# The last sub-tile of an FFT and feed-forward kernel, made in two column halves

## The chip, the cores and the metric

The kernel runs on one core of one Trainium2 chip. The metric is the device time of one execution in microseconds, taken over several runs; lower is better. Beside the timed runs, one execution of each kernel was profiled. The profiled *span*, from the first to the last instruction of the program, is 1.7 to 2.2 us shorter than the time.

## The reference

```python
# x: 8 x 3008 x 256
X = rfft(x, axis=1)
Yr = Xr @ w_r - Xi @ w_i + b_r ;  Yi = Xr @ w_i + Xi @ w_r + b_i
Yr, Yi = soft_threshold(Yr, 0.01), soft_threshold(Yi, 0.01)
y = irfft(Yr + 1j * Yi, n=3008, axis=1).reshape(24064, 256)
h = y @ w_in                       # 256 -> 2048
g = s * relu(h) ** 2 + b
out = g @ w_out                    # 2048 -> 256, float32
```

Only the last line matters here: the end of its last tile of 512 tokens.

## The kernel before

The feed-forward part goes tile by tile, 512 tokens each. The second product of a tile is made sub-tile by sub-tile (128 tokens, 256 output columns, 16 accumulating matmuls). Two sub-tiles share a bank of PSUM (the memory into which TensorE accumulates) and one evacuation (VectorE copies the result from PSUM to SBUF, the on-chip memory, and applies `s` and the bias on the way); a store goes out for each sub-tile. In the last tile, sub-tiles 2 and 3 are already handled alone so that less work hangs on the end.

```python
apool = ctx.enter_context(tc.tile_pool(name="psa", bufs=2, space=bass.MemoryType.PSUM))
opool = ctx.enter_context(tc.tile_pool(name="op", bufs=3))
# ... cut ...
def other_bank():
    return apool.tile([P, 512], F32, name="psa", tag="psa")
# ... cut ...
        if kind == "main":                                   # in store(tl, sub, src)
            rows = out[b * N + 512 * j : b * N + 512 * (j + 1), :]
            rows = rows.rearrange("(n1 n2) d -> n2 n1 d", n2=N2)[8 * sub : 8 * sub + 8]
            nc.sync.dma_start(out=rows, in_=src)
            return
# ... cut ...
        def mm(sub, mc):                                     # in second_mms(ti)
            alone = ti == len(tiles) - 1 and sub >= 2
            h = 0 if alone else sub % 2
            if h == 0 and mc == 0:
                hold["ps"] = other_bank().rearrange("p (h e) -> p h e", h=2)
            ps = hold["ps"]
            nc.tensor.matmul(
                ps[0:size, h, :], gts[(ti, mc // 2)][:, mc % 2, sub * size : (sub + 1) * size],
                w_out_t[:, mc, :],
                start=(mc == 0), stop=(mc == MC - 1),
            )
            # ... cut ...
            if mc == MC - 1 and (alone or h == 1 or sub == nsub - 1):
                k = h + 1
                ost = opool.tile([P, 2, D], F32, name="ost", tag="ost")
                nc.vector.scalar_tensor_tensor(
                    out=ost[0:size, 0:k], in0=ps[0:size, 0:k], scalar=s_bc[0:size],
                    in1=bias_bc[0:size].unsqueeze(1).to_broadcast([size, k, D]), op0=ALU.mult, op1=ALU.add,
                )
                load["dve"] += 0.12 + 0.27 * k
                for i in range(k):
                    store(tl, sub - k + 1 + i, ost[:, i, :])
```

The line to keep in mind is `bufs=3`: evacuated tiles take turns in three buffers of SBUF, and a buffer can be written again only when every store that reads it has landed. The framework in which the kernel is written puts in those waits by itself; nothing in the code shows them.

## Time and profile before

| | before |
|---|---|
| median of 3 runs, before the change was tried | 846.8 us (846.79 to 846.98) |
| profiled span | 844.56 us |
| TensorE busy | 835.1 us, 99% |
| last matmul ends | 840.47 us |
| from there to the end (the *tail*) | 4.10 us |

How to read it: TensorE works without a gap almost to the end, so the only stretch where other engines and the DMA set the time is the tail. The tail is a line of single steps: evacuation of the last sub-tile (VectorE), issue of its store (the SyncE queue, SPq), landing of the store (its last semaphore increment), closing. In the profile lines PE is TensorE, PEld its weight loads, DVE VectorE, DVEq and SPq the instruction queues of VectorE and SyncE. The lines that show this stand in the prediction.

### The profile page before, as it was taken

Reading aid. Unit: us, or ns where it says so; the run is one execution under the profiler, and the core shown is the slowest. Engines: PE = TensorE matmul, PEld = TensorE weight load, DVE = VectorE, ACT = ScalarE, POOL = GpSimd, SP = SyncE. Lnnn points to the kernel's source line nnn. Section 1 sums busy time; section 2 is a strip of 40 time slices with the busy share of each in tenths; the row PEclk is TensorE's granted clock in tenths of the full one; section 3 lists DMA queues with packets and bytes.
Section 4 is the critical chain, followed back from the end, with each engine's and each line's share of the span. In section 5 each row is a group of like instructions: output and inputs, shape, how many; then the busy total and the mean of one; then the engine's idle time right before and its main releaser. Section 6 shows DMA issues by size and latency. Waiting matters only on the chain.

```text
span 844.6 us, 17119 instructions
## 1 busy us (share of the span) xinstructions
PE 835.1 (99%) x6654; PEld 601.3 (71%) x6654; DVE 694.7 (82%) x1034; ACT 640.6 (76%) x862; POOL 45.9 (5%) x73
## 2 busy tenths in 40 slices
PE   8999999999999999999999999999999999999998
PEld 7857767777677766777677776777667777766765
DVE  5999987888888988888888888798978888776674
ACT  5987887778778877788777787778877778666673
POOL 4630000000000001000000000000000000000000
PEclk9999999999999999999999999999999999999999
DMA  7955467224851367324761247613354223411111
GB/s 200 181 151 118 119 161 199 74 77 98 202 156 54 103 171 188 93 70 107 189 174 50 81 101 196 172 43 90 106 152 125 59 78 97 113 33 38 38 44 50
DMA packets 105939, 96.06 MB, mean 114 GB/s; under 512 B 9607, under 2 KB 97675, under 8 KB 104515
## 3 DMA queue, kind: packets, MB, share of 16 engines
q1 hardware_dynamic: 99362, 80.55, 32.9%
q0 software_dynamic: 6496, 14.42, 10.6%
q8 instruction: 52, 0.85, 0.4%
q14 instruction: 29, 0.23, 0.1%
HBM read 53.52 MB, written 46.66 MB: 119 GB/s over the span
## 4 chain that ended last, share of the span: by engine, by line
PE 92%; ACT 3%; DVE 2%; DMA 1%; issue 1%; POOL 0%; DVEq 0%; ACTq 0%; POOLq 0%
PE psa L852 38%; PE psh L781 37%; PE psf L647 4%; PE psf L582 3%; PE psf L633 2%; PE psf L677 2%; PE psf L618 2%; PE psf L730 2%; ACT rt L788 1%; DMA x<-in_x_dram 1%; PE psm L425 1%; POOL x L213 0%; ACT yt L170 0%; DVE z L463 0%; PE psf L456 0%
## 5 line engine op out<-in xcount | busy, mean ns | idle before, releaser
L788 ACT ACTIVATE rt<-psh 128x1024 f32<-128x1024 f32 (+2 forms) x384 | 387.2, 1009 | 120.2 <-PE psh L781 118.8
L795 DVE TENSOR_TENSOR gt<-rt 128x1024 f16<-128x1024 f32 (+2 forms) x319 | 382.3, 1202 | 94.4 <-ACT rt L788 93.4
L852 PE MATMUL psa<-w_out_t,gt 128*128 128x256 f16 (+1 forms) x3024 | 454.4, 272 | 0.1
L852 PEld LDWEIGHTS <-gt 128*128 128x128 f16 (+1 forms) x3024 | 300.9, 101 | 186.6 <-issue 1.1
L781 PE MATMUL psh<-yt,w_in 128*128 128x512 f16 (+1 forms) x1344 | 396.8, 378 | 0.2 <-ACT rt L788 0.2
L781 PEld LDWEIGHTS <-w_in 128*128 128x128 f16 x1536 | 142.7, 98 | 26.2 <-issue 1.2
L862 DVE SCALAR_TENSOR_TENSOR ost<-psa,s_bc,bias_bc 128x512 f32<-128x512 f32 (+2 forms) x97 | 71.1, 733 | 9.6 <-PE psa L852 7.9
L792 ACT ACTIVATE gt<-rt 128x1024 f16<-128x1024 f32 (+2 forms) x65 | 68.2, 1050 | 0.9
L652 DVE TENSOR_TENSOR ring<-psf,s 128x512 f16<-128x512 f32 x84 | 57.6, 685 | 3.3 <-PE psf L647 3.2
L170 ACT CAST v<-psf 128x512 f16<-128x512 f32 x77 | 44.8, 582 | 19.4 <-PE psf L677 19.4
L170 ACT CAST xf<-psf 128x512 f16<-128x512 f32 x79 | 46.3, 586 | 8.8 <-PE psf L618 8.8
L781 PE MATMUL psh<-tail,w_in 128*128 128x512 f16 (+1 forms) x192 | 52.1, 353 | 0.0
L170 ACT CAST u<-psf 96x512 f16<-96x512 f32 x74 | 42.8, 580 | 11.2 <-PE psf L582 10.9
L647 PE MATMUL psf<-W_g,xf 128*128 128x256 f16 x336 | 50.4, 273 | 0.0
L170 ACT CAST yt<-psf 128x480 f16<-128x480 f32 (+2 forms) x76 | 39.0, 520 | 14.7 <-PE psf L730 14.2
L213 POOL DMA_DIRECT2D x<-in_x_dram x36 | 18.8, 527 | 432.9 <-PE psf L582 431.7
L582 PE MATMUL psf<-x,A_t 94*96 94x512 f16 x102 | 38.9, 382 | 1.0 <-ACT yt L170 0.6
L658 DVE TENSOR_TENSOR ring<-ring,high 128x512 f16<-128x512 f16 x84 | 35.6, 423 | 2.3
L659 DVE TENSOR_TENSOR ring<-ring 128x512 f16<-128x512 f16 x84 | 35.6, 423 | 2.1
L657 DVE TENSOR_TENSOR ring<-ring,low 128x512 f16<-128x512 f16 x84 | 35.5, 422 | 1.6
L647 PEld LDWEIGHTS <-xf 128*128 128x128 f16 x336 | 32.9, 98 | 4.1 <-issue 0.2
L730 PE MATMUL psf<-C_t,vs 96*128 96x96 f16 x448 | 33.2, 205 | 0.0
(100 smaller groups left out, 508.6 us busy)
## 6 DMA issues: line engine op xcount, KB each, us to landing
out_dram<-ost SPq DMA_DIRECT2D x152, 128.0 KB
ud<-u SPq DMA_DIRECT2D x28, 384.0 KB
us<-ud SPq DMA_DIRECT2D x28, 384.0 KB
vd<-v SPq DMA_DIRECT2D x42, 256.0 KB
vs<-vd SPq DMA_DIRECT2D x14, 768.0 KB
x<-in_x_dram POOLq DMA_DIRECT2D x28, 376.0 KB, 6.3
ring<-ring SPq DMA_DIRECT2D x280, 32.0 KB
out_dram<-ost SPq DMA_DIRECT2D x16, 120.0 KB
```

Source lines behind the costliest of these rows:

```text
L170: return None, nc.scalar.copy(out=dst, in_=src)
L582: nc.tensor.matmul(ps[0:96, :], A_t[0:N1, :], x16[(b, c)][0:N1, j * D : (j + 2) * D], start=True, stop=True,)
L647: nc.tensor.matmul(ps[:, r, :], xt[:, 2 - r, dc], W_g[:, dc, r], start=(dc == 0), stop=(dc == DC - 1),)
L652: nc.vector.tensor_tensor(out=t, in0=ps, in1=hold[i // 2][:, i % 2].unsqueeze(1).to_broadcast([P, 2, D]), op=ALU.add,)
L658: nc.vector.tensor_tensor(out=m, in0=m, in1=high, op=ALU.min)
L730: nc.tensor.matmul(ps[:, j * 96 : (j + 1) * 96], vs[(b, h)][:, k, ec * P : (ec + 1) * P], C_t, start=True, stop=True,)
L781: nc.tensor.matmul(o, w_in_t[dc][:, mc * P : (mc + 1) * P], r, start=(dc == 0), stop=(dc == DC - 1),)
L788: nc.scalar.activation(out=rt[:, :, 0:w], in_=ps[:, :, 0:w], func=AF.Relu)
L792: nc.scalar.activation(out=gt[:, :, 0:w], in_=rt[:, :, 0:w], func=AF.Square)
L795: nc.vector.tensor_tensor(out=gt[:, :, 0:w], in0=rt[:, :, 0:w], in1=rt[:, :, 0:w], op=ALU.mult)
L852: nc.tensor.matmul(ps[0:size, h, :], gts[(ti, mc // 2)][:, mc % 2, sub * size : (sub + 1) * size], w_out_t[:, mc, :], start=(mc == 0), sto ...
L862: nc.vector.scalar_tensor_tensor(out=ost[0:size, 0:k], in0=ps[0:size, 0:k], scalar=s_bc[0:size], in1=bias_bc[0:size].unsqueeze(1).to_broad ...
```

## The change

The intent is to shorten that line. Sub-tile 3 of the last tile is made in two groups of 128 columns. The first group can be evacuated and stored while the second is still on TensorE, so that after the last matmul only half a sub-tile is left to evacuate and store.

```diff
-    def store(tl, sub, src):
+    def store(tl, sub, src, e=slice(None)):
...
-            nc.sync.dma_start(out=rows, in_=src)
+            nc.sync.dma_start(out=rows[:, :, e], in_=src)
...
+        def mm_last(c, mc):
+            if mc == 0:
+                hold["ps"] = other_bank()
+            ps, sub = hold["ps"], nsub - 1
+            e = slice(c * P, c * P + P)
+            nc.tensor.matmul(
+                ps[0:size, 0:P], gts[(ti, mc // 2)][:, mc % 2, sub * size : (sub + 1) * size],
+                w_out_t[:, mc, e], start=(mc == 0), stop=(mc == MC - 1),
+            )
+            if mc == MC - 1:
+                ost = opool.tile([P, P], F32, name="ost", tag="ost")
+                nc.vector.scalar_tensor_tensor(
+                    out=ost[0:size], in0=ps[0:size, 0:P], scalar=s_bc[0:size],
+                    in1=bias_bc[0:size, e], op0=ALU.mult, op1=ALU.add,
+                )
+                store(tl, sub, ost, e)
+
+        if ti == len(tiles) - 1:
+            units = [lambda s=s, m=m: mm(s, m) for s in range(nsub - 1) for m in range(MC)]
+            return units + [lambda c=c, m=m: mm_last(c, m) for c in range(2) for m in range(MC)]
```

Below, A is the evacuation of sub-tiles 0 and 1 of the last tile (with its stores A1 and A2), B that of sub-tile 2, C that of sub-tile 3; C0 and C1 are its halves.

## The prediction

> **What bounds the kernel now.** I read the page from the top, then went to the last ten microseconds, since the change touches nothing else. The page says that TensorE is busy from end to end and that the chain that ended last is mostly TensorE:
>
> ```profile
> PE 835.1 (99%) x6654; PEld 601.3 (71%) x6654; DVE 694.7 (82%) x1034; ACT 640.6 (76%) x862; POOL 45.9 (5%) x73
> ...
> PE 92%; ACT 3%; DVE 2%; DMA 1%; issue 1%; POOL 0%; DVEq 0%; ACTq 0%; POOLq 0%
> ```
>
> The reader is to see that no work off TensorE is worth anything before the tail. The change adds or removes no work in the first 838 us; its whole effect must lie in the tail, where TensorE has run dry. So I took the chain of waits for 836 to 845 us and, for VectorE, the order of time in the same stretch:
>
> ```profile
> 835.99 4.49 PE psa L852 x41
> 840.48 0.02 issue
> 840.50 0.48 DVE ost L862
> ```
>
> ```profile
> 837.45 0.75 DVE L862 SCALAR_TENSOR_TENSOR ost<-psa,s_bc,bias_bc 128x512 f32<-128x512 f32 x1 [2.23 <-PE psa L852]
> 838.76 0.48 DVE L862 SCALAR_TENSOR_TENSOR ost<-psa,s_bc,bias_bc 128x256 f32<-128x256 f32 x1 [0.56 <-PE psa L852]
> 840.50 0.48 DVE L862 SCALAR_TENSOR_TENSOR ost<-psa,s_bc,bias_bc 128x256 f32<-128x256 f32 x1 [1.26 <-PE psa L852]
> ```
>
> These are the three evacuations of the last tile: A (sub-tiles 0 and 1 together, 837.45), B (sub-tile 2, 838.76), C (sub-tile 3, 840.50). Each is followed by stores, read from the DMA issues in order of time. A's two stores are issued at 838.23 and 838.87, B's at 839.58, C's last:
>
> ```profile
> 841.02 0.60 SPq L814 DMA_DIRECT2D out_dram<-ost  x1
> ```
>
> The trace's record of semaphore increments (not printed on the page) gives the landings of these four stores: 840.88, 841.77, 842.53 and 843.64. So the end is a line of single steps: matmuls until 840.48, evacuation C 0.48, store C 841.02 to 843.64 (2.62 us), and closing barriers to 844.56 (0.92). The DMA view of 841.5 to 844.6 us (40 slices of 0.0775 us) agrees:
>
> ```profile
> DMA  5555322101336253555544100000000000000000
> ```
>
> Seven busy slices are B's data; C's begin near 842.2, 1.2 us after its issue, and end near 843.3. The run that was profiled took 846.51 us for a span of 844.56; I carry that constant 1.95 us along, and predict differences.
>
> **What the Trainium skill says.** "Perfetto Trace Analysis", Per-instruction lifecycle (its hardware-generated DMA instruction): the profile shows a store only until its descriptors are pushed, and the data movement is outside. The trace agrees: the store's bar is 0.60 us, its landing comes at 2.62. "DMA: Bandwidth & Descriptors", Anatomy of one DMA: a constant near 2 us, mostly the write receipt, so halving a small store saves little (its fit is for the other issue path). Here 128 descriptors of 1 KB land in 2.61 at least, 112 in 2.50, 56 in 2.39: agreement on the flatness. "TensorE: Matmul & The Clock Gate", the section asking why 56 ns and not 53.3: successive matmuls of 128 columns start 55 to 56 ns apart on a warm clock. The trace agrees: five warm-up matmuls of 128 columns near 6 us span 0.44 with the last lasting 0.218, so (0.44 - 0.218) / 4 = 55.5 ns, each with its own weight load; 256 columns run at 4.49 / 41 = 109.5. "VectorE: DVE Perf Modes", the errata table, has 120 + columns cycles from PSUM; for 256 that is 392 ns by its clock, and the trace has 485, so I use the trace.
>
> **The change, part by part.** The last sub-tile's 16 matmuls of 256 columns become two groups of 16 of 128 columns, each with its own PSUM bank, evacuation, and store of 128 rows of 512 bytes.
>
> *Matmuls.* 16 x 109.5 = 1.75 us become 32 x 55.5 = 1.78. The first half (C0) ends near 839.61, the second (C1) near 840.5. Weight loads double, but the warm-up and the 96-column matmuls show they don't limit. Cost +0.03 at most. Banks: there are two; C1's is B's, read out by 839.24, before C1 starts at 839.6. No wait.
>
> *Evacuations.* 512 columns take 0.745 and 256 take 0.485, so a column costs 0.260 / 256 = 1.02 ns and the constant is 0.225: 128 columns take 0.355. The one on the path gets 0.13 shorter. C0's, from 839.62 to 839.98, lies beside C1's matmuls.
>
> *Stores.* C0's waits for B's issue (to 840.19, then a semaphore instruction), runs 840.27 to 840.87 and lands near 842.9, off the path. C1's issue could start at 840.93 at best. The descriptor count stays 128, so I keep 0.60 for the issue; packets are shorter (the trace's 512-byte packets take 27 ns, its 1 KB ones 46; some 8 per queue, so 0.15 saved). I estimate 2.5 from issue to landing.
>
> *If nothing else happened*, the sum would be 840.50 + 0.355 to 840.86, issue 840.93, landing 843.43, end 844.35: a gain of 0.2 us, 846.6. That's the intent.
>
> *The output buffer.* The pool for the evacuated tiles (tag `ost`) has three buffers. Counting back: before, C's buffer was last used by the previous tile's second pair, stored at 834.11 and 834.76 and landed by 837.75, so C waits for nothing. After, the last four uses are A, B, C0, C1: C1 is the fourth and gets the buffer of A. A smaller tile under the same tag still takes a whole buffer. So C1's evacuation must wait until both stores of A have landed, 841.77, whereas its matmuls are ready at 840.5. That wait is 1.27 us. The trace shows that evacuations carry such waits already, as separate semaphore instructions ahead of them, though so far they cost nothing:
>
> ```profile
> L862 DVEq EVENT_SEMAPHORE  x125: 21/50/50, 61.1 to 838.8; - x125
> ```
>
> A is not made earlier by the change and its stores stay first in the queue, so 841.77 stands. Then: 841.77 + 0.07 (the wait's own instruction and start) = 841.84; evacuation 0.355 to 842.20; issue at 842.23; landing 2.5 later, 844.73; barriers 0.92, end 845.65. Against 844.56 that is **1.1 us more**. As a sum over the path: wait +1.34, evacuation -0.13, store -0.12, matmuls at most +0.03, hidden in the wait. With rounding I add 1.0 to the median of 846.8: **847.8 us**.
>
> **The rivals.** *No wait, a small gain.* If the allocator gave the smaller tiles space of their own, or the wait were on something already done, the time would be 846.6. The memory of three buffers under one tag speaks against it; the intent speaks for it. I give it one in ten.
>
> *The DMA issue becomes the bound.* The stores A1, A2, B, C0, C1 are 0.60 each on one queue. From 838.23, with the gap for B's evacuation, C0's ends at 840.87, only just before C1 would need it. Without the buffer wait this costs 0.05 or so; with it, the queue is idle by then. Worth under 0.1.
>
> *A2's landing moves.* It took 2.89 from issue here, and the last tiles' second stores took 2.70 to 2.99. That makes C1's start 841.57 to 841.87, and the time 847.6 to 847.9. If C0's data slowed A2's, it would be later, but C0's data start only near 841.45, when A2's are nearly through. *Stores of 512-byte rows slower than I think*: many short transfers of that size land quickly in this trace; at the old 2.62 the time is 847.9.
>
> **Range and chances.** With the wait the terms spread over 847.5 to 848.1, and two runs of one kernel differ by 0.2. Another chip can shift both. The tail below covers part of the no-wait case. I take 847.0 to 848.5. Two per cent is 17 us, several times the tail that the change touches (4 us from the last matmul on), so within 2% has 0.99, and the rest is for mishaps.
>
> **What would show each step right or wrong.** In the changed trace: (1) 32 matmuls of 128 columns in about 1.78 us, with the end of the last near 840.5 on the old time line; (2) two evacuations of 128x128 of about 0.355 each; (3) between them a gap on VectorE of nearly 2 us, the second starting just after the second of A's stores lands, not after the last matmul; (4) five stores instead of four in the tail, the last issued near 842.2 and landing about 2.5 later; (5) everything before 838 unchanged. The prediction is wrong if the second evacuation starts within 0.1 us of the last matmul, if the store of half the bytes is over 0.3 faster or slower than the whole one, or if the order of instructions elsewhere has shifted.

## The result and the profile after

| | before | changed |
|---|---|---|
| median of 6 runs | 846.80 us (846.37 to 847.73) | 847.88 us (847.51 to 850.21) |
| profiled span | 844.56 | 845.71 |
| last matmul ends | 840.47 | 840.38 |
| tail | 4.10 | 5.33 |

The ratio of the changed kernel to the one before is 1.0015, with a 95% interval of 1.0002 to 1.0028: within 2%, and slower by a little over one microsecond. A ratio here is the mean time of one kernel's runs over the mean of the other's in the same rounds, so it isn't quite the ratio of the medians.

VectorE in order of time, changed kernel, 836 to 846 us (columns: start, duration, engine, line, operation, and in brackets the idle time before it with what ended it):

```profile
838.63 0.48 DVE L862 SCALAR_TENSOR_TENSOR ost<-psa,s_bc,bias_bc 128x256 f32<-128x256 f32 x1 [0.56 <-PE psa L852]
839.52 0.35 DVE L882 SCALAR_TENSOR_TENSOR ost<-psa,s_bc,bias_bc 128x128 f32<-128x128 f32 x1 [0.41 <-PE psa L876]
841.83 0.35 DVE L882 SCALAR_TENSOR_TENSOR ost<-psa,s_bc,bias_bc 128x128 f32<-128x128 f32 x1 [1.95 <-DMA out_dram<-ost]
```

These are B, C0 and C1. C0 was released by TensorE, C1 by a store (`DMA out_dram<-ost`) after 1.95 us of idle time. Before, all three last evacuations had been released by TensorE.

The chain of waits of the same stretch names the store:

```profile
837.32 0.76 DVE ost L862
838.08 0.02 issue
838.10 0.60 SPq L814
838.70 0.04 issue
838.75 2.96 DMA out_dram<-ost
841.71 0.03 issue
841.73 0.05 DVEq L882
841.78 0.04 issue
841.83 0.35 DVE ost L882
```

Read it backwards. C1 at 841.83 waited for a semaphore instruction (DVEq), that for a store that was issued at 838.75 and took 2.96 us to land; the queue had been busy with another store at 838.10, and both read what was evacuated at 837.32. That evacuation is A. Before, this stretch of the chain was nothing but matmuls.

TensorE in order of time, changed kernel, shows that the work itself is hardly longer than it was (before, the 16 whole-width matmuls span 1.91 us):

```profile
838.43 1.95 PE L876 MATMUL psa<-w_out_t,gt 128*128 128x128 f16 x32
```

The 32 half-width matmuls span 1.95 us, the recorded 0.22 of the last one included; start to start they are 56 ns.

The tail, step by step, from the trace (start and end of instructions, and the last semaphore increment of the last store):

| us | before | changed | difference |
|---|---|---|---|
| end of last matmul to start of last evacuation | 0.04 | 1.45 | +1.41 |
| last evacuation | 0.48 | 0.35 | -0.13 |
| its end to the issue of its store | 0.03 | 0.03 | 0 |
| issue of the last store to its landing | 2.62 | 2.15 | -0.47 |
| landing to end of the program | 0.93 | 1.36 | +0.43 |
| sum (rounded) | 4.10 | 5.33 | +1.23 |

The first two rows were predicted. The store and the closing were not: the half store lands faster than estimated, and the closing takes longer though nothing in the change was meant for it. The experiments ask for all three causes.

### The profile page after: what moved, and what is told of

Same layout as the page of the kernel before. It is cut to its first block, busy times and chain, and to the rows that moved or that the text cites. A ratio compares the mean times of both kernels' runs of the same rounds, so it can differ in the third digit from the quotient of the medians.

```text
span 845.7 us, 17156 instructions
## 1 busy us (share of the span) xinstructions
PE 833.5 (99%) x6670; PEld 599.5 (71%) x6670; DVE 694.7 (82%) x1035; ACT 640.6 (76%) x862; POOL 46.0 (5%) x73
## 4 chain that ended last, share of the span: by engine, by line
PE 92%; ACT 3%; DVE 2%; DMA 1%; issue 1%; POOL 0%; SPq 0%; DVEq 0%; ACTq 0%; POOLq 0%
PE psh L781 37%; PE psa L852 37%; PE psf L647 4%; PE psf L582 3%; PE psf L633 2%; PE psf L677 2%; PE psf L618 2%; PE psf L730 2%; ACT rt L788 1%; DMA x<-in_x_dram 1%; PE psm L425 1%; POOL x L213 0%; ACT yt L170 0%; DVE z L463 0%; PE psf L456 0%
## 5 line engine op out<-in xcount | busy, mean ns | idle before, releaser
L862 DVE SCALAR_TENSOR_TENSOR ost<-psa,s_bc,bias_bc 128x512 f32<-128x512 f32 (+1 forms) x96 | 70.6, 735 | 8.3 <-PE psa L852 6.7
L170 ACT CAST u<-psf 96x512 f16<-96x512 f32 x74 | 42.8, 580 | 11.2 <-PE psf L582 10.9
```

The source lines that it names most:

```text
L170: return None, nc.scalar.copy(out=dst, in_=src)
L862: nc.vector.scalar_tensor_tensor(out=ost[0:size, 0:k], in0=ps[0:size, 0:k], scalar=s_bc[0:size], in1=bias_bc[0:size].unsqueeze(1).to_broad ...
```

## The experiments

All runs gave correct results. The tail of each comes from its own trace. The kernel before ran beside them in the same rounds, 11 times in each of two batches, each on a chip of its own (own, bufs2, shift1 and own_shift7 ran in the first batch, the others in the second): median 846.59 (846.11 to 847.69) and 846.62 (846.13 to 850.22).

| kernel | evacuations wait for a store? | last store: issue to landing | landing to end | tail | median time | ratio to before, 95% interval |
|---|---|---|---|---|---|---|
| before | no | 2.62 | 0.93 | 4.10 | see above | 1 |
| changed | yes | 2.15 | 1.36 | 5.33 | 847.88 | 1.0015 (1.0002 to 1.0028) |
| own | no | 2.33 | 1.34 | 4.16 | 848.53 | 1.0020 (1.0005 to 1.0034) |
| own_again | no | 2.47 | 1.36 | 4.31 | 846.96 | 1.0005 (0.9990 to 1.0020) |
| bufs2 (whole width) | yes | 3.02 | 0.93 | 5.87 | 848.18 | 1.0017 (1.0004 to 1.0030) |
| shift1 (whole width) | no | 2.94 | 1.34 | 4.83 | 847.98 | 1.0025 (1.0009 to 1.0041) |
| after_shift7 | yes | 2.13 | 0.91 | 4.77 | 846.82 | 1.0003 (0.9990 to 1.0016) |
| own_shift7 | no | 2.49 | 0.92 | 3.89 | 846.10 | 0.9996 (0.9984 to 1.0008) |
| one_tile | no | 2.69 | 1.35 | 4.51 | 847.53 | 1.0012 (0.9997 to 1.0027) |
| one_tile_shift7 | no | 2.29 | 0.92 | 3.69 | 846.81 | 1.0002 (0.9987 to 1.0018) |

**The halves in buffers of their own (own, own_again).**

```diff
-                ost = opool.tile([P, P], F32, name="ost", tag="ost")
+                ost = opool.tile([P, P], F32, name="ost_h", tag="ost_h", bufs=2)
```

> The changed kernel, with the two half-width tiles in two buffers of their own. Theory (the second half waits for the buffer of the first pair): VectorE's wait for the stores is gone, the second half's evacuation starts within 0.05 us of its last matmul instead of 1.4 us after it, and the span falls by 1.0 to 1.4 us from the changed kernel's 845.7, to 844.3 to 844.7, which is the kernel before within 0.3. Rival (the halves themselves cost it: more matmuls, one more store on the queue): the span stays near 845.7.

VectorE in order of time, the two halves of `own`:

```profile
839.92 0.35 DVE L882 SCALAR_TENSOR_TENSOR ost_h<-psa,s_bc,bias_bc 128x128 f32<-128x128 f32 x1 [0.41 <-PE psa L876]
840.81 0.35 DVE L882 SCALAR_TENSOR_TENSOR ost_h<-psa,s_bc,bias_bc 128x128 f32<-128x128 f32 x1 [0.54 <-PE psa L876]
```

With only the buffers changed, the second half is released by TensorE, 0.04 us after its last matmul, and the tail falls from 5.33 to 4.16. (The span, 844.93, lies 0.2 above the range expected, since the last matmul ended 0.40 later than in the changed kernel's profile.) This rules out the rival that the halves themselves cost the time. But the timed runs disagreed with the profile: 846.5 to 851.0, a median of 848.53. So the same kernel was run again.

> The same kernel as in the run with buffers of its own, again, since its profile showed a tail as short as before's while its timed runs scattered from 846.5 to 851.0. If the scatter belongs to the chip at that moment, the median comes near the kernel before's, within 0.5; if it belongs to the kernel, the median is again over 1.5 us above.

The second batch gave 846.82 to 848.62, a median 0.34 us above before's, with a tail of 4.31. That meets the expectation, so the scatter seems to belong to the runs and not to the kernel: in that second batch two runs of the kernel before took 850.22 and 849.55. But the second batch ran on another chip, so it can't tell the moment from the chip. The runs over 849.5 us whose granted clock was listed had a mean of 0.995 or 0.996 (0.998 for the 850.21 of the changed kernel), where the quickest had 0.999 or 1.000; single runs near 846.6 had 0.997 too, so the clock isn't all of it. What lowers the clock in some runs stays open. The profiles show two places ahead of the tail where runs part: the first 55 us (by then `shift1` and `one_tile` are 0.6 us behind the profile of before) and a wait of TensorE for a load (`us<-ud`) near 544 us, which is there in `own_again` and `bufs2` and not in before. This scatter is why a few tenths of a microsecond are read from the traces here and not from medians.

**The wait alone, without halves (bufs2).** The kernel before with one buffer fewer, so that its whole-width C must wait for A's buffer as C1 does in the changed kernel.

```diff
-    opool = ctx.enter_context(tc.tile_pool(name="op", bufs=3))
+    opool = ctx.enter_context(tc.tile_pool(name="op", bufs=2))
```

> The kernel before, whole width, with two output buffers instead of three, so that its last evacuation too must wait for the stores of the first pair. Theory: the wait alone makes all of the loss; the last evacuation starts near 841.8 instead of 840.5 and the span grows by 1.2 to 1.4 us to about 845.9, with no halves at all. Rival: under 0.3 us more. It also tells what sets a store's landing, since here a store of whole rows is issued with the queue empty: 2.6 us if its bytes set it, 2.15 us (as the second half's took in the changed kernel) if being alone sets it.

VectorE in order of time, its C:

```profile
842.82 0.48 DVE L862 SCALAR_TENSOR_TENSOR ost<-psa,s_bc,bias_bc 128x256 f32<-128x256 f32 x1 [2.64 <-DMA out_dram<-ost]
```

The last matmul ended at 841.41, so C starts 1.41 us after it instead of 0.04: 1.37 more, where the changed kernel has 1.41 more, and this without any halves. The tail grew by 1.77, more than the 1.2 to 1.4 expected, and the rest is the store, which took 3.02 us to land where before's took 2.62. The span, 847.3, was 1.4 above the 845.9 expected: 0.4 of it is this store, and nearly all the rest arose before the tail, since the last matmul ended 0.94 later than in the profiled run of before. Two buffers also made four early evacuations wait for a transfer (1.3 us of idle VectorE in all, in the first 300 us). These did not delay TensorE: against the profile of before it is 0.06 us behind at 494 us, and 0.9 more comes from the one wait for `us<-ud` near 544 us. Whether two buffers have a part in that wait is not shown (`own_again`, with three, has it too, 0.4 long).

This run also tells what sets a landing. Three DMA views of equal length (3.5 us in 40 slices of 0.0875 us; each digit is the busy share of the 16 DMA engines in tenths), each with the last store's data as its last busy group. First before, 841 to 844.5 us; its last store was issued at 841.02:

```profile
DMA  4455545454221024535355553200000000000000
```

Then the changed kernel, 842.2 to 845.7 us, issue at 842.21:

```profile
DMA  2100000000000024455400000000000000000000
```

Then bufs2, 843.3 to 846.8 us, issue at 843.33:

```profile
DMA  0000000000000315434464554200000000000000
```

In all three the data begin some 14 slices, 1.24 us by the trace's records of single packets, after the issue. (The first digit of bufs2's group, a 3, is an instruction load of 0.49 us and not the store.) The two whole stores are then busy for 12 slices, bufs2's with a few nearly idle ones after them; the half store for 6. The packet records, from the first start to the last end, give 1.04, 1.32 and 0.55 us. After the last packet 0.33 to 0.45 us pass until the landing. So the halved bytes, in the same 128 packets, about halve the data's time (31 ns a packet instead of 57 to 59), and being alone in the queue doesn't do it: bufs2's store is alone as well and takes no less than before's. That it took 0.40 us more is one straggler: seven of its eight semaphore increments were there by 845.92, 2.59 us after the issue, and the last came at 846.35. The instruction load, which began at 844.49, just ahead of the data, is the likely reason; this isn't shown.

**The closing (shift1).** In the changed kernel the instructions after the landing are semaphore waits of the SyncE queue, one after the other. The program uses eight DMA semaphores in turn for the hardware queue, and the closing waits look at them in a fixed order. In the kernel before, the last store had the semaphore that is looked at last; all others had been passed while it was still on its way. The changed kernel has one store more, so its last store had the next semaphore in the turn, which is looked at second. The waits for the seven others then come after the landing: in the changed kernel they start at 844.43 and end at 844.83, 0.06 us each. Two lines of the waits of the SyncE queue from 841 us on show the difference, (us in total, times, longest us), first before, where the store before the last and the last one each end a wait, then changed, where one wait of 1.5 us is ended by a store and no later one is:

```profile
SPq L947 <- DMA out_dram<-ost: 1.5, 2, 1.1
```

```profile
SPq L968 <- DMA out_dram<-ost: 1.5, 1, 1.5
```

To test this on the kernel before, one load of four bytes was put on the same queue, which moves all later transfers of that queue one semaphore on. The code asks for it in mid-kernel, and so do the expectations; in the traces the loads are issued near the start (at 4.9 us here, from 4.4 to 10.9 us where there are seven). The order of the queue's other transfers stays the same.

```diff
+    shift = [cpool.tile([1, 1], F32, name=f"shift_{i}") for i in range(1)]
+    for i, t in enumerate(shift):
+        plan.setdefault(300 + 20 * i, []).append(
+            lambda t=t: nc.sync.dma_start(out=t, in_=moe_s.unsqueeze(0))
+        )
```

> The kernel before with one load of 4 bytes added on the same queue in mid-kernel, which moves every later DMA one semaphore on in the rotation. Theory of the closing: the last store now takes the semaphore that the closing waits look at second instead of last, the seven later waits of 0.06 us each come after the landing, and the span grows by about 0.4 us (landing to end 1.3 instead of 0.92). Rival: the closing is a constant 0.92 and the longer closing of the changed kernel was chance or came from its own order of instructions; span 844.6 within 0.15.

Landing to end became 1.34 us instead of 0.93, as expected: a load that has nothing to do with the tail costs 0.41 us in it. The span was 845.87, not the 845.0 expected. Of the excess, 0.32 is this run's landing of the last store (2.94 us for the same store that took 2.62 before), and the last matmul ended 0.57 later, all of which was there by 55 us (the kernels with seven loads have no such delay). Neither bears on the closing.

**Both repaired (own_shift7).** The kernel of `own` with seven such loads, so that its last store has the semaphore that is looked at last.

```diff
+    shift = [cpool.tile([1, 1], F32, name=f"shift_{i}") for i in range(7)]
+    # ... the same loop
```

> The changed kernel with buffers of its own for the halves and seven loads of 4 bytes in mid-kernel, so that its last store takes the semaphore that is looked at last. Theory of the closing: landing to end 0.92 instead of 1.3, so 0.4 us under the run without the seven loads, 843.9 to 844.3, the first version below the kernel before's 844.6. Rival: no difference to that run.

Landing to end is 0.92 and the span 844.33, about as expected, and the tail 3.89, the first below before's 4.10. Against `own` the tail lost 0.27, not 0.42, since the last store took 0.16 longer to land. The median, 846.10, is 0.49 under before's of the same rounds, but the interval of the ratio (0.9984 to 1.0008) contains 1.

**The closing alone (after_shift7).** The changed kernel as it is, wait included, with the seven loads.

> The changed kernel, with the buffer wait left in, and seven loads of 4 bytes in mid-kernel so that its last store takes the semaphore that the closing looks at last. Theory of the closing: landing to end 0.92 instead of 1.36, so the stretch from the last matmul to the end is 4.9 us instead of 5.33; the wait for the first pair's stores stays near 1.9 us of VectorE idle. Rival: 5.3 as before the loads.

VectorE in order of time, its last evacuation:

```profile
841.76 0.35 DVE L882 SCALAR_TENSOR_TENSOR ost<-psa,s_bc,bias_bc 128x128 f32<-128x128 f32 x1 [1.85 <-DMA out_dram<-ost]
```

The wait for A's store is still there (1.85 us of idle time) and the landing is unchanged (2.13), but landing to end is 0.91 and the tail 4.77 instead of 5.33. Of these 0.56, the closing is 0.44 and a shorter wait 0.10 (1.35 after the last matmul instead of 1.45). So the closing changes with the wait in place, as it did without it.

**Both halves in one buffer (one_tile).** No buffer is added; the halves go side by side into one.

```diff
-                ost = opool.tile([P, P], F32, name="ost", tag="ost")
+                if c == 0:
+                    hold["o"] = opool.tile([P, 2, D], F32, name="ost", tag="ost")
+                ost = hold["o"][:, 0, e]
```

> The changed kernel with both halves evacuated into the two halves of one buffer, no memory added. Theory of the buffer: one buffer fewer is asked for, so the second half waits for nothing that is late; last matmul to end 4.1 to 4.2 us as with buffers of its own, with the closing still 1.34. Rival: the two writes into one buffer, or the store that reads the first half, hold up the second evacuation; 5 us or more.

C1 starts 0.04 us after its last matmul, so the wait is gone without any memory. The tail, 4.51, was above the 4.1 to 4.2 expected; the store's landing, 2.69, is the term that was long, and the step from the last matmul to the issue was as in `own`.

**One buffer and the shifted closing (one_tile_shift7).**

> One buffer for both halves, and the seven loads. Theory: both costs gone, last matmul to end 3.8 to 3.9 us, 0.2 to 0.3 under the kernel before's 4.10; time about 0.3 to 0.5 us under the kernel before of the same rounds. Rival: no better than the kernel before.

```profile
840.28 0.35 DVE L884 SCALAR_TENSOR_TENSOR ost<-psa,s_bc,bias_bc 128x128 f32<-128x128 f32 x1 [0.54 <-PE psa L876]
```

The tail is 3.69 us and the profiled span 843.93, the shortest of all. The expectation for the time failed, though: the median of the six runs is 846.81, not under before's 846.62, with an interval of 0.9987 to 1.0018. Its six runs lie between 845.70 and 849.64. So the trace shows a tail 0.4 us shorter than before's, and the timed runs can't tell the kernels apart.

Nor do the timed runs show that taking the wait away gives the microsecond back: own, own_again and one_tile, without the wait, took 848.53, 846.96 and 847.53, and the changed kernel 847.88 in rounds of its own. What is shown here is shown in the tails of the profiles, one profile for each run.

## Why the prediction was right

- **The bound.** Right. The work of TensorE ends within 0.1 us of the same time (840.38 against 840.47), and the order of its matmuls before the tail is the same; all of the difference is in the tail.
- **Matmuls.** Right: 56 ns start to start against the 55.5 predicted; no wait for a PSUM bank, no limit by weight loads.
- **Evacuations.** Right: 0.351 us against 0.355.
- **The output buffer.** Right, and it is the cause of the loss. C1 started after A2's landing at 841.71, predicted 841.77, and evacuated from 841.83, predicted 841.84. Shown by taking the wait away in two ways (`own` and `one_tile`, each also with the shifted closing) and by making it alone (`bufs2`, +1.37 us on that step).
- **The store.** Most of the latency is constant, as predicted, but the term was mis-sized: "I estimate 2.5 from issue to landing"; it took 2.15 here and 2.13 in after_shift7. That is 0.47 under the whole store, so this step failed by the prediction's own sign ("over 0.3 faster or slower than the whole one"). The estimate took 0.15 off for shorter packets. The packet records show what was overlooked: the data's own time is 1.04 us for before's whole store and 0.55 for the half. They also don't bear out that the constant is "mostly the write receipt": 1.24 us pass before the first packet and 0.33 to 0.45 after the last. Queued close behind C0's store (five profiles), the half took 2.29 to 2.69: its first packet came 1.41 to 1.59 us after the issue, and its data took 0.56 to 0.75. So the gain depends on what is ahead of it. These are single observations of something that moved by 0.4 us between runs (whole: 2.62 to 3.02).
- **The closing.** "Barriers 0.92" failed as a constant: it was 1.36. The position of the last store's semaphore in the closing's order decides it, shown by `shift1` in one direction and by the three kernels with seven loads in the other. No step of the prediction took that position into account.
- **The sum.** Predicted 1.1 us on the span, measured 1.15. The last two points, -0.35 and +0.43, nearly cancel. The close agreement of the total is thus in part luck, while the main term is not. In the time there is more luck: the prediction made 1.0 of its 1.1 us "with rounding", and allowed 0.2 us for scatter where the six timed runs of the kernel before lie 1.4 apart and those of the changed kernel 2.7, one of them (850.21) outside the range.
- **The rivals.** No wait: did not happen. The queue as the bound: not seen with the wait; with the wait removed, the issue of C1's store came 0.10 us after its evacuation instead of 0.03 (in `own`, 841.16 to 841.26); the 0.07 more lies within the 0.05 to 0.1 that was allowed. A2's landing moved by 0.06.

## What to carry to other kernels

When a piece of work is cut into more pieces, count what else goes by pieces: a pool of three buffers that had always been early enough was one short by the last half, and the wait took more than the halving gave. At the very end of a program count the steps one by one, the closing included, and check a total that fits by its terms. When an expected gain is a few tenths of a microsecond in 847, the trace can show the mechanism, but timed runs that scatter by more can't confirm the gain.

## What the Trainium skill lacked or had wrong

- "DMA: Bandwidth & Descriptors", Anatomy of one DMA: its fit adds bytes / 436e3 us to a constant, which would make, as an estimate, 0.15 us for the 64 KB saved. (The page gives it for the software path.) On the hardware queue here the half store's data took 0.50 us less and it landed 0.47 us sooner than before's last store (0.87 sooner than bufs2's), with the same 128 packets.
- "VectorE: DVE Perf Modes", the errata table: 120 + columns cycles from PSUM give, as an estimate by its clock, 258 ns for 128 columns. The runs show 351 for 128, 484 for 256 and 745 to 750 for 512: the slope agrees (1.02 to 1.04 ns a column), the constant here is about 0.22 us instead of 0.125.
- "Perfetto Trace Analysis", Optimization Strategy: it speaks of missing buffers as bubbles that repeat. Here, in the changed kernel, the shortage made one bubble of 1.95 us on VectorE, at the end alone, and none before.
- None of the pages that I read tells that the closing of a program waits for the DMA semaphores in a fixed order, so that the one taken by the last store sets 0.92 or 1.36 us after its landing.
